# Three pads and a tile shift that set where 256-column moving operands start

## The chip, the core and the metric

The kernel runs on one core of a Trainium2 chip. The metric is device time in microseconds of one execution, from three executions of the kernel; the trace comes from a further execution that was profiled.

## The reference

Retention attention (scores weighted by a decay, no softmax) over 4 batches, 8 heads, 576 positions and 64 dimensions gives 2304 tokens of 512 features. Two MLPs follow. Cut to what matters:

```python
ret = (q @ k.T) / sqrt(64) * Dmat          # Dmat = gamma_h ** (i - j) for i >= j, else 0
x   = (ret @ v)                            # as (2304, 512)
h   = relu(x @ w_in)                       # 512 -> 2048
x   = (h * h) @ w_out                      # 2048 -> 512
g   = x @ w_gate                           # 512 -> 1536
out = (silu(g) * (x @ w_val)) @ moe2_w_out # 1536 -> 512
```

Weights of the MLPs arrive as 64-bit words on the device (the kernel rounds them to float32 itself).

## The kernel before, in words

Every float32 operand of the MLPs is split into a high and a low part, and each product is made of three matmuls in float32r: high weights by high data, high by low, low by high. The helper `three` (L235, L236, L237) issues them; the last MLP's output product (`o_piece`, L1285 to L1287) issues its own three. A matmul here has a stationary operand of 128 columns, that is 512 bytes in each partition, and a moving operand of 512, 384 or 256 columns (2048, 1536 or 1024 bytes in each partition).

The order on TensorE is fixed by a chain (`pe` makes every TensorE step depend on the one before). The stages are:

- 0 to about 148 us: attention chunks among the first token block of the first MLP (512 columns: operands `x`, then `h`).
- about 148 to 219 us: the second token block, which has only 256 tokens: matmuls `hps<-x,w` (`mlp1_h`) and `acc<-h,w` (`mlp1_y`), all of 256 columns, with attention chunks between them.
- to about 470 us: three more token blocks. Their first product is done by a Strassen-like scheme (`mlp1_s`): seven products of 256 columns for each pair of weight tiles (`gv<-xb,w` and `hps<-xb,w`, weights partly from `sx`), with the second product (512 columns, `acc<-h,w`) in pieces between them.
- to the end: the second MLP. Its first two products have 384 columns (`gv<-xc,w`), and between them stand pieces of the output product of 256 columns (`acc<-w,at`, `hps<-w,at`, `gv<-w,at`), where the weight tile is the moving operand and the activations `at` are stationary.

Memory in a partition is handed out by pools in the order in which they are opened, so the width of a pad tile moves all tiles behind it. `pad3` stands ahead of the attention's pools, `pad4` between `xs` and `sx`, and `pad6` between the last MLP's `xc`, `rg` and its `at`. `shift(n)` leaves some floats unused at the front of `x` (L507, in `new_x`) and of `h` (in `mlp1_act`) where a block has fewer than 512 tokens.

In the built program the start of the moving operand minus the start of the stationary one, modulo 512 bytes, is 0 for all float32r matmuls of 512 and 384 columns and 192 for all of 256 columns (192 `x`, 192 `h`, 1008 `xb` and 1134 `w` by `at` matmuls). The first 144 matmuls of the first token block, in pieces of 384 and 128 columns, also start at 0.

Of the kernel before, what the change touches and what calls it, by code (L numbers as in the profile page):

```python
# [10 lines left out]
F32 = mybir.dt.float32  # L11
# [181 lines left out]
def kernel(ctx: ExitStack, tc: tile.TileContext, units, qtab, tab, w1, w2, out):  # L193
# [277 lines left out]
    late, hps_free = {}, {}  # L471
# [1 line left out]


    astack = ExitStack()
    astack.enter_context(tc.tile_pool(name="pad3", bufs=1)).tile([128, 208], F32, name="pad3")
    xp = astack.enter_context(tc.tile_pool(name="xp", bufs=1))
    up = astack.enter_context(tc.tile_pool(name="up", bufs=1))
    ap_ = astack.enter_context(tc.tile_pool(name="ap", bufs=1))
# [19 lines left out]

    def shift(n):  # L500

        return 48 if n < 512 else 0

    def new_x(j):
        n = BLOCKS[j][1] * C
        t = (x1 if j else xp).tile([128, KC * 2 * n + shift(n)], F32R, tag="x", name="x")
        X[j] = t[:, shift(n):].rearrange("p (k a n) -> p k a n", k=KC, a=2)  # L507
# [208 lines left out]
    def mlp1_act(j, f):  # L716
# [16 lines left out]
        def hi():  # L733
            t = hp.tile([128, 2 * n + shift(n)], F32R, tag="h", name="h")
            Hs[j, f] = t[:, shift(n):].rearrange("p (a n) -> p a n", a=2)
            nc.scalar.copy(out=Hs[j, f][:, 0], in_=st["r"])
# [719 lines left out]
    def swap():  # L1456
        astack.close()
        late["tl"] = ctx.enter_context(tc.tile_pool(name="tl", bufs=1, reuse_waits="tile"))
        for key in ("xb", "xs", "pad4", "sx"):
            late[key] = bstack.enter_context(tc.tile_pool(name=key, bufs=7 if key == "xb" else 1, reuse_waits="tile"))  # L1460
        late["pad4"].tile([128, 80], F32, name="pad4")
        late["S"] = late["sx"].tile([128, 2, HALF1], F32R, tag="sx", name="sx")
        pgv = ctx.enter_context(tc.tile_pool(name="pgv", bufs=1, space=PSUM, reuse_waits="tile"))
        late["MA"], late["MB"], more = (pgv.tile([128, 512], F32, name=f"gv{i}") for i in range(3))
        late["more"] = [banks[0], more]

    def swap2():
        wstack.close()
        for key, bufs in (("xc", NX), ("rg", 1), ("pad6", 1), ("at", NAT), ("tm", 1), ("gg", 1)):
            late[key] = ctx.enter_context(tc.tile_pool(name=key, bufs=bufs, side="right", reuse_waits="tile"))  # L1470
        late["pad6"].tile([128, 48], F32, name="pad6")

    def swap3():
        bstack.close()
# [6 lines left out]
    for j in range(PLAIN_BLOCKS):  # L1481
        at = dict(zip(INSERTS[j], range(cell, NC)))
        cell += len(at)
        for f in range(NF1):
# [13 lines left out]
            if c is not None:  # L1498
# [5 lines left out]
                if c + 1 < NC:  # L1504
                    att_load(c + 1, 40)
    do.named["open"] = do("NONE", 0.0, swap, [*(lo_op[c] for c in range(NC)), h_op[0, NF1 - 1], f_last[2], *(st_op[c] for c in range(NC))])
    sum_loads()
    pieces = mlp1_y(*pend, apart=True)
    for j in range(PLAIN_BLOCKS, NB):
        if j > PLAIN_BLOCKS:  # L1510
            fetch_x1(j, -1)
        for p in range(NF1P):
            if p == 1:
                for _ in range(LATER.get(j, 0)):
                    convert2()
            pieces = [*mlp1_s(j, p, pieces), *mlp1_y(j, 2 * p, apart=True), *mlp1_y(j, 2 * p + 1, apart=True)]
    late["open2"] = do("NONE", 0.0, swap2, [y_op[NB - 1, NA - 1], N_op[NB - 1, NA // 2, 5]])
    late["open3"] = do("NONE", 0.0, swap3, [late["open2"], ("ysdone", 0), "lowxs", N_op[NB - 1, NF1P - 1, 6]])
    while todo:
# [3 lines left out]
    for b in range(N2):  # L1523
# [13 lines left out]
        for f in range(NF2):  # L1537
# [9 lines left out]
            n = len(mine)  # L1547
# [94 lines left out]
```

## Time and profile before

| | |
|---|---|
| median of three executions | 862.42 us (862.01 to 864.3) |
| profiled execution, its own time | 866.6 us |
| its span, first to last instruction | 864.8 us |
| TensorE busy share of the span | 99% |
| mean granted TensorE clock | 0.996 |

A matmul's row has a start and a duration; durations overlap, since matmuls are pipelined. What a matmul costs in a dense stream is the distance from its start to the next one's start, called the spacing here. It is read from the timeline as the time between two rows divided by the number of matmuls from one to the other.

### The profile page before, as it was taken

What the parts mean: (1) busy time and instruction counts of PE and PEld (TensorE: products, weight loads), DVE (VectorE), ACT (ScalarE), POOL (GpSimd) and SP (SyncE); (2) the same over time, 40 slices, a digit from 0 to 9 for tenths busy, and PEclk for the clock granted to TensorE, in tenths of its full rate; (3) what the DMA queues carried; (4) which work ended last, traced back from release to release, by engine and by line L of the source; (5) the groups of instructions that cost most, each with busy time, mean ns of one, the idle gap of its engine ahead of it and who ended that gap; (6) DMA issues with size and microseconds to landing.
All of it is one profiled execution on the core that took longest, in us unless ns stands there. A gap on an engine that the chain in (4) does not pass through costs nothing.

```text
span 864.8 us, 15867 instructions
## 1 busy us (share of the span) xinstructions
PE 853.8 (99%) x5990; PEld 804.0 (93%) x5990; DVE 628.0 (73%) x1034; ACT 506.7 (59%) x994; POOL 134.7 (16%) x141
## 2 busy tenths in 40 slices
PE   8999999999999999999999999999999999999998
PEld 6878888989999999999998999999999999999998
DVE  5799987646677857785788778588666688656675
ACT  3577774437877877887887444365333355333353
POOL 3121127651223022212310201000000000000000
PEclk9899999999999999999999999999999999999999
DMA  9587879999989789969899898978867788776782
GB/s 369 206 329 268 305 268 315 387 379 301 316 297 329 267 288 346 315 233 329 281 342 385 300 402 296 392 259 308 318 227 263 261 261 281 276 260 223 267 265 74
DMA packets 113084, 254.83 MB, mean 295 GB/s; under 512 B 8560, under 2 KB 67696, under 8 KB 103664
## 3 DMA queue, kind: packets, MB, share of 16 engines
q1 hardware_dynamic: 113008, 253.82, 83.5%
q8 instruction: 47, 0.77, 0.4%
q14 instruction: 29, 0.24, 0.1%
HBM read 195.59 MB, written 58.20 MB: 293 GB/s over the span
## 4 chain that ended last, share of the span: by engine, by line
PE 92%; DMA 5%; ACT 1%; DVE 1%; issue 0%; SPq 0%; DVEq 0%
PE gv L235 13%; PE gv L237 13%; PE gv L236 13%; PE acc L237 7%; PE acc L236 7%; PE acc L235 7%; PE acc L1285 4%; PE acc L1287 4%; PE acc L1286 4%; PE hps L235 4%; PE hps L237 4%; PE hps L236 4%; PE sc L577 1%; DMA raw<-w 1%; DMA qk<-units 1%; DMA w<-ws 1%
## 5 line engine op out<-in xcount | busy, mean ns | idle before, releaser
L235 PE MATMUL gv<-xc,w 128*128 128x384 f32 x504 | 169.4, 336 | 0.2 <-ACT u L1133 0.2
L237 PE MATMUL gv<-xc,w 128*128 128x384 f32 x504 | 168.9, 335 | 0.0
L236 PE MATMUL gv<-xc,w 128*128 128x384 f32 x504 | 168.7, 335 | 0.0
L236 PE MATMUL acc<-h,w 128*128 128x512 f32 (+1 forms) x320 | 117.3, 367 | 0.0
L237 PE MATMUL acc<-h,w 128*128 128x512 f32 (+1 forms) x320 | 117.3, 367 | 0.0
L235 PE MATMUL acc<-h,w 128*128 128x512 f32 (+1 forms) x320 | 117.3, 367 | 0.0
L453 POOL TENSOR_TENSOR f<-f 128x256 f32<-128x256 f32 x72 | 61.9, 859 | 274.2 <-DVE cw L410 181.5
L235 PEld LDWEIGHTS gv<-xc,w 128*128 128x128 f32 x504 | 94.6, 188 | 1.3 <-ACT u L1133 0.6
L236 PEld LDWEIGHTS gv<-xc,w 128*128 128x128 f32 x504 | 94.6, 188 | 0.1
L237 PEld LDWEIGHTS gv<-xc,w 128*128 128x128 f32 x504 | 94.6, 188 | 0.0
L1287 PE MATMUL acc<-w,at 128*128 128x256 f32 x288 | 81.0, 281 | 0.0
L1285 PE MATMUL acc<-w,at 128*128 128x256 f32 x288 | 80.9, 281 | 0.0
L1286 PE MATMUL acc<-w,at 128*128 128x256 f32 x288 | 80.9, 281 | 0.0
L237 PEld LDWEIGHTS acc<-h,w 128*128 128x128 f32 x320 | 60.1, 188 | 10.0
L235 PE MATMUL gv<-xb,w 128*128 128x256 f32 x238 | 67.1, 282 | 0.0
L237 PE MATMUL gv<-xb,w 128*128 128x256 f32 x238 | 66.8, 281 | 0.0
L236 PE MATMUL gv<-xb,w 128*128 128x256 f32 x238 | 66.8, 281 | 0.0
L236 PEld LDWEIGHTS acc<-h,w 128*128 128x128 f32 x320 | 60.1, 188 | 6.4
L235 PEld LDWEIGHTS acc<-h,w 128*128 128x128 f32 x320 | 60.1, 188 | 6.4
L927 DVE TENSOR_TENSOR h<-g,h 128x256 fp32r<-128x256 f32 x96 | 47.9, 499 | 19.1 <-ACT h L923 18.2
L1145 DVE TENSOR_TENSOR m<-gv,m 128x384 f32<-128x384 f32 x36 | 20.1, 558 | 53.5 <-PE gv L237 53.5
L1133 ACT COPY m<-gv 128x384 f32<-128x384 f32 x72 | 34.5, 479 | 40.7 <-PE gv L237 40.2
(174 smaller groups left out, 2094.9 us busy)
## 6 DMA issues: line engine op xcount, KB each, us to landing
w<-wdS SPq DMA_DIRECT2D x36, 1024.0 KB, 5.5
raw<-w SPq DMA_DIRECT2D x34, 1024.0 KB, 7.5
w<-wdP SPq DMA_DIRECT2D x36, 768.0 KB, 7.3
w<-ws SPq DMA_DIRECT2D x94, 256.0 KB, 5.0
w<-wdOP SPq DMA_DIRECT2D x54, 256.0 KB, 5.4
w<-wdOS SPq DMA_DIRECT2D x18, 768.0 KB, 7.5
ws<-cw SPq DMA_DIRECT2D x16, 512.0 KB, 8.5
wdS<-cw SPq DMA_DIRECT2D x12, 512.0 KB, 6.3
```

The costliest lines, as they stand in the source:

```text
L235: nc.tensor.matmul(ps, lhsT=wh, rhs=xh, start=first, stop=False, skip_group_check=onto)
L236: nc.tensor.matmul(ps, lhsT=wh, rhs=xl, start=False, stop=False, skip_group_check=onto)
L237: nc.tensor.matmul(ps, lhsT=wl, rhs=xh, start=False, stop=last, skip_group_check=onto)
L453: nc.gpsimd.tensor_tensor(out=w[:, o], in0=w[:, x], in1=w[:, y], op=op)
L577: nc.tensor.matmul(s[h][:, p], lhsT=A[c][r, p, 1], rhs=A[c][r, p, 0], start=True, stop=True)
L927: nc.vector.tensor_tensor(out=t[:, 1, half], in0=st[key][:, half], in1=t[:, 0, half].bitcast(F32), op=ALU.subtract)
L1133: nc.scalar.copy(out=st[name], in_=late[bank][:, :HALF])
L1145: nc.vector.tensor_tensor(out=st["m5"], in0=late["MA"][:, :HALF], in1=st["m5"], op=ALU.add)
L1285: nc.tensor.matmul(ps, lhsT=ah, rhs=wh, start=product not in ONTO and q == 0 and off == 0, stop=False, skip_group_check=True)
L1286: nc.tensor.matmul(ps, lhsT=ah, rhs=wl, start=False, stop=False, skip_group_check=True)
L1287: nc.tensor.matmul(ps, lhsT=al, rhs=wh, start=False, stop=q == NQ - 1, skip_group_check=True)
```

## The change

`shift` gives 16 floats (64 bytes) instead of 48 (192 bytes) for blocks of fewer than 512 tokens. `pad3` and `pad4` become 32 floats (128 bytes) longer, `pad6` 32 floats shorter. In the built program every moving operand of 256 columns then starts 64 bytes past its stationary operand modulo 512; the matmuls of 512, 384 and 128 columns keep their difference. Three kinds of tile carry it: the operands `x` and `h` of the second block start 128 bytes earlier in their tiles, `xb` lies 128 bytes lower, and `at` lies 128 bytes higher. With them the result tiles `m1`, `u2`, `m5`, `rs` and `st` move down, and `g` and `sg` up, each by 128 bytes. All instructions stand in the same order on all engines as before, with the same sizes and waits.

```diff
-    astack.enter_context(tc.tile_pool(name="pad3", bufs=1)).tile([128, 208], F32, name="pad3")
+    astack.enter_context(tc.tile_pool(name="pad3", bufs=1)).tile([128, 240], F32, name="pad3")
...
-        return 48 if n < 512 else 0
+        return 16 if n < 512 else 0
...
-        late["pad4"].tile([128, 80], F32, name="pad4")
+        late["pad4"].tile([128, 112], F32, name="pad4")
...
-        late["pad6"].tile([128, 48], F32, name="pad6")
+        late["pad6"].tile([128, 16], F32, name="pad6")
```

## Rows read from the trace of the kernel before

**Rows 1.** The page: engines, busy us (share of the span), instructions.
```profile
PE 853.8 (99%) x5990; PEld 804.0 (93%) x5990; DVE 628.0 (73%) x1034; ACT 506.7 (59%) x994; POOL 134.7 (16%) x141
```

**Rows 2.** Waits of TensorE after 225 us: us in total, times, longest.
```profile
PE gv L235 <- ACT u L1133: 0.2, 1, 0.2
```

**Rows 3.** Stages: window, us, busy (count) by engine, granted clock, DMA share, GB/s.
```profile
148.00:225.00 77.00, 75.53 (x769) 72.25 (x768) 44.57 (x74) 44.04 (x96) 32.54 (x35) 1.00 1.00 351
225.00:473.00 248.00, 247.76 (x1552) 225.10 (x1551) 185.00 (x312) 198.97 (x434) 50.58 (x58) 1.00 0.89 310
473.00:560.00 87.00, 87.00 (x548) 86.71 (x548) 64.91 (x117) 38.69 (x75) 7.82 (x10) 1.00 0.95 346
560.00:865.00 305.00, 301.76 (x2051) 301.27 (x2049) 211.25 (x385) 131.57 (x271) 0.00 (x0) 1.00 0.73 254
```

**Rows 4.** 256-column matmuls by line and shape: count | busy us, mean ns | idle.
```profile
L237 PE MATMUL hps<-x,w 128*128 128x256 f32 x64 | 17.7, 277 | 0.0
L236 PE MATMUL acc<-h,w 128*128 128x256 f32 x64 | 17.7, 277 | 0.0
...
L237 PE MATMUL gv<-xb,w 128*128 128x256 f32 x238 | 66.8, 281 | 0.0
...
L235 PE MATMUL hps<-xb,w 128*128 128x256 f32 x94 | 26.4, 281 | 0.0
...
L1286 PE MATMUL acc<-w,at 128*128 128x256 f32 x288 | 80.9, 281 | 0.0
...
L1287 PE MATMUL hps<-w,at 128*128 128x256 f32 x54 | 15.2, 281 | 0.0
...
L1285 PE MATMUL gv<-w,at 128*128 128x256 f32 x36 | 10.1, 281 | 0.0
```

**Rows 5.** Timeline of TensorE, 256 columns, second block: first and last of 191.
```profile
194.30 0.28 PE L236 MATMUL hps<-x,w 128*128 128x256 f32 x1
...
215.84 0.28 PE L237 MATMUL gv<-xb,w 128*128 128x256 f32 x1
```

**Rows 6.** The same, last MLP: first and last of 101 of 256 columns.
```profile
572.15 0.28 PE L1285 MATMUL acc<-w,at 128*128 128x256 f32 x1
...
583.92 0.28 PE L1286 MATMUL hps<-w,at 128*128 128x256 f32 x1
```

**Rows 7.** The same: 512 columns and the 256 on both sides.
```profile
242.19 0.28 PE L235 MATMUL gv<-xb,w 128*128 128x256 f32 x1
...
242.89 0.39 PE L235 MATMUL acc<-h,w 128*128 128x512 f32 x1
...
244.25 0.28 PE L235 MATMUL hps<-xb,w 128*128 128x256 f32 x1
```

**Rows 8.** The same: 256 columns and 384 behind them, an ordinary place.
```profile
761.49 0.28 PE L1285 MATMUL acc<-w,at 128*128 128x256 f32 x1
...
762.91 0.34 PE L235 MATMUL gv<-xc,w 128*128 128x384 f32 x1
763.08 0.34 PE L236 MATMUL gv<-xc,w 128*128 128x384 f32 x1
...
764.82 0.34 PE L237 MATMUL gv<-xc,w 128*128 128x384 f32 x1
```

**Rows 9.** The same place 10 us later, behind one longer step.
```profile
770.22 0.34 PE L237 MATMUL gv<-xc,w 128*128 128x384 f32 x1
770.39 0.35 PE L235 MATMUL gv<-xc,w 128*128 128x384 f32 x1
770.58 0.34 PE L236 MATMUL gv<-xc,w 128*128 128x384 f32 x1
770.76 0.34 PE L237 MATMUL gv<-xc,w 128*128 128x384 f32 x1
770.93 0.28 PE L1285 MATMUL acc<-w,at 128*128 128x256 f32 x1
...
772.30 0.34 PE L235 MATMUL gv<-xc,w 128*128 128x384 f32 x1
```

## The prediction

> **What bounds the kernel now.** I read the engines' shares first. TensorE is busy for 853.8 of 864.8 us [rows 1], and the reader should see that no other engine comes near it. Then its waits: after 225 us there is one, of 0.2 us [rows 2]. So TensorE's stream sets the end, and what counts is the spacing of its matmuls, from start to start. The granted clock is 1.00 in all four stages behind 148 us [rows 3], which is the level of 2.4 GHz, and so 256 columns alone would take 106.7 ns, 384 would take 160.0 and 512 would take 213.3.
>
> The timeline gives the spacings. In the second block 191 matmuls of 256 columns stand in one unbroken run from 194.30 to 215.84 us, 190 steps: 113.4 ns each [rows 5]. In the last MLP 101 of the same width run from 572.15 to 583.92, 100 steps: 117.7 ns each [rows 6]. I call these the lower and the upper spacing. Both runs start their moving operands 192 bytes past the stationary ones, so this offset alone does not fix the spacing. The profile's mean durations tell the two apart over the whole kernel: 277 ns for the groups of the second block and 281 ns for all large groups behind it [rows 4]. The matmuls of 512 columns take 6 steps from 242.89 to 244.25, 226.7 ns each [rows 7], and those of 384 take 10 steps from 763.08 to 764.82, 174 ns each [rows 8]. Beyond their columns' own time that is 13.4 and 14 ns, at an offset of 0; the 256-column ones pay 6.7 ns at the lower spacing and 11.0 at the upper.
>
> What decides between the two spacings? DMA traffic does not: the lower one stands in the stage where the DMA share is 1.00, the upper one where it is 0.73 [rows 3]. The rows point to the state in which a run is entered. Twelve matmuls from 761.49 to 762.91, entered from an even stream of 384 columns, take 118.3 ns each [rows 8]. Twelve at 770.93 take 114.2 ns [rows 9]; the stream ahead of them was jolted by one step of 190 ns (770.39 to 770.58) where about 174 is usual. Once entered, a spacing stays: 100 steps in a row did not leave the upper one [rows 6]. I read this as two streams, the moving operand's reads and the next weights' reads, that lock into one of two patterns. That reading is inferred, not shown.
>
> **The change part by part.** It adds and removes no instruction, and it moves none past another on any engine or queue. What it changes is where 2526 matmuls read.
>
> First, 1008 matmuls of `xb` and 1134 of `w` by `at`. By their groups' mean durations nearly all run at the upper spacing [rows 4]: three lines of 238, 94, 288, 54 and 36 are 2130 matmuls. About 75 of them still run at the lower spacing (those at the start of the `xb` stage, where the run of [rows 5] ends, and the twelve of [rows 9]), and about 55 of the second block run at the upper one, so I count 2110. If 64 bytes bring these to the lower spacing, 2110 x (117.7 - 113.4) ns = 9.1 us, and with the finer value of the triples, 353.3 against 340 ns (or 13.3 ns a triple, what [rows 6] and [rows 5] give within their rounding), 9.4 us. I take 9.3. All of it lies on the path that sets the end, since TensorE waits for nothing there [rows 2].
>
> Second, the second block's 384 matmuls and the 75 at the start of the next stage, some 390 at the lower spacing already. They can gain nothing that the trace shows and can lose the same step, 390 x 4.4 ns = 1.7 us.
>
> The bounds of the unknown spacing at 64 bytes: below, the lower spacing of 113.4 ns, the nearest row of the same shape [rows 5]. Above, the 13.3 ns beyond the columns that the shapes at an offset of 0 pay [rows 7, 8], which is 120.0 ns; 64 bytes lie nearer to that offset than 192 do. I take the lower one, because the same instructions already run at it in two places and a single jolt was enough to get there [rows 5, 9], so it needs only that the entry from 384 or 512 columns falls otherwise. That is a choice, not a proof.
>
> Third, the cover. If TensorE gains 9.3 us over some 640 us, what feeds it must come 1.5% faster. The narrowest place is 473 to 560 us, with a DMA share of 0.95 [rows 3], where TensorE still waits for nothing [rows 2]; about 160 of the 256-column matmuls lie there, so at most 160 x 4.4 ns = 0.7 us can be given back. VectorE and ScalarE are busy for 185 and 199 of the 248 us of the `xb` stage [rows 3], which leaves more than the gain of some 4 us. The result tiles that move by 128 bytes are read and written by those engines, which are not the bound; I cost that at nothing, with their idle time as the cover, and at most the 0.7 us above if it is gone.
>
> Against the change stands a rule. The Trainium skill, "TensorE: Matmul & The Clock Gate", section "Step-by-step: what each phase is for", says that TensorE has two independent read ports, so that loading the next tile's weights steals nothing from the running matmul. By it no offset between the two operands can matter and the sum is 0. The trace agrees only in part: it has two spacings for one shape at one offset, 113.4 and 117.7 ns, which the rule does not give.
>
> Sum: the profiled execution took 866.6 us, of which 864.8 is span; 866.6 - 9.3 = 857.3. It lies 4.2 us above the median of 862.42. The same difference from the median gives **853.1 us**.
>
> **The rivals.** *Half the gap.* The upper spacing may be a mixture (its triple of 353.3 ns lies two steps of 6.67 ns above 340), and one of the two steps may go: 2110 x 2.2 ns = 4.7 us, so 857.7 us. For it: the sizes 6.7 and 13.4 ns beyond the columns are one and two such steps [rows 5, 7]. Against it: no run of the trace shows 115.5 ns.
>
> *No effect.* Entry and pattern are set by how long the weights of the next matmul have been waiting, not by addresses: a 256-column run behind 512 or 384 columns is then at the upper spacing whatever the offset. For it: at one offset both spacings occur, and every ordinary entry from longer matmuls gives the upper one [rows 7, 8]. Against it: a jolt with no wait at all gave the lower one [rows 9]. It gives 862.4 us, or 864.1 if the second block alone loses its lower spacing. The rule of the two read ports leads to the same time.
>
> *Slower.* 64 bytes lie closer to the point at which both streams read the same place modulo 512, and each weights load then costs the moving stream two steps of 6.67 ns instead of one, as it does at offset 0 for 512 and 384 columns [rows 7, 8]. Then the 2110 go from 117.7 to 120.0 ns, 4.9 us, and the 390 at the lower spacing go up by 6.6 ns, 2.6 us: 862.4 + 7.5 = 869.9 us; 867.3 if only the first happens. It decides wherever the spacing of dense 256-column runs is above 117.7 ns. For it: every row at an offset of 0 pays 13 to 14 ns. Against it: those rows have other widths, and their next weights are loaded long before they end.
>
> **How the numbers follow.** The lower spacing everywhere: 0.28, about 853.1 us. Half the gap: 0.17, about 857.7. No effect, with or without the second block's loss: 0.25, 862.4 to 864.1. Slower: 0.30, 867.3 to 869.9. A time within 0.3% (2.6 us) can't be told from no change in a measurement of this kernel. So faster is 0.28 + 0.17 = 0.45, same 0.25, slower 0.30. The likeliest single case gives the time. The range runs from 852 (the whole gain and 1 us more) to 868, which takes in the milder half of the slower case and leaves out the other, about 0.15, and 0.05 below. Cases of both signs hold most of the chance; the likeliest one's own range is 852 to 855.
>
> **What would show it.** Right: the groups of [rows 4] that now have a mean of 281 ns read 277, a run like that of [rows 6] has 113.4 ns a step, and the rows of 384 and 512 columns keep 174 and 226.7. Half: 115 to 116 ns a step. No effect: 281 and 117.7 again. Slower: durations above 281 ns and about 120 ns a step, in the second block too. The forecast is also wrong, with the mechanism right, if the faster stream finds a wait between 473 and 560 us: TensorE's waits behind 225 us would then be above 0.2 us, with a DMA as the releaser.

## The result, and the profile after

The changed kernel took 870.23 us (869.9 to 870.81, four executions) against 863.36 us (862.01 to 865.36, four) for the kernel before: a ratio of 1.008, with a 95% interval of 1.0062 to 1.0099. It is slower by 0.8%, where 853.1 us had been forecast, and 870.23 lies above the range's upper end of 868.

The two profiled executions stand closer together. They have the same mean granted clock, 0.996, and their spans are 868.5 and 864.8 us, 3.7 us apart. The windows below cut both spans at the same points of the program: the first 256-column matmul of `x`, of `xb`, and the first of `xc`. The columns are the window, its length and TensorE's busy time with its matmuls, the weight loads, VectorE, ScalarE, GpSimd, the granted clock, the DMA share and GB/s. These points lie a few us ahead of the round figures for the stages given above. First the kernel after:

```profile
145.30:213.70 68.40, 67.39 (x690) 64.20 (x689) 39.17 (x60) 34.49 (x70) 31.69 (x31) 1.00 1.00 350
213.70:460.30 246.60, 246.60 (x1568) 223.23 (x1568) 179.65 (x307) 198.29 (x444) 52.55 (x60) 1.00 0.88 302
460.30:868.50 408.20, 404.91 (x2677) 402.49 (x2675) 289.19 (x524) 182.16 (x363) 9.49 (x12) 1.00 0.79 278
```

The kernel before, cut at the same points:

```profile
145.30:212.90 67.60, 66.13 (x691) 63.01 (x690) 37.82 (x60) 34.24 (x70) 31.70 (x33) 1.00 1.01 354
212.90:456.80 243.90, 243.90 (x1568) 222.50 (x1567) 180.32 (x307) 197.92 (x444) 52.37 (x60) 1.00 0.88 304
456.80:864.80 408.00, 404.73 (x2677) 402.30 (x2675) 289.11 (x524) 182.11 (x363) 9.50 (x12) 1.00 0.79 279
```

Both reach the second block at 145.3 us. From there the second block lost 0.8 us, the `xb` stage 2.7 and the last stage 0.2: 3.7 in all. The other engines are busy in each stage for the same time within 1.5 us, the DMA shares agree within 0.01, and behind 225 us TensorE still has the one wait of 0.2 us, as in [rows 2]:

```profile
PE gv L235 <- ACT u L1133: 0.2, 1, 0.2
```

So it is the spacing again. TensorE's timeline of the kernel after: 186 matmuls of the second block and the start of the `xb` stage, answering to [rows 5]; a stretch of the `xb` stage with six matmuls of 512 columns and six of 256, answering to [rows 7]; and 97 matmuls of the last MLP, answering to [rows 6].

```profile
194.08 0.28 PE L236 MATMUL hps<-x,w 128*128 128x256 f32 x1
...
215.87 0.28 PE L235 MATMUL gv<-xb,w 128*128 128x256 f32 x1
...
236.47 0.39 PE L235 MATMUL acc<-h,w 128*128 128x512 f32 x1
...
237.85 0.28 PE L235 MATMUL gv<-xb,w 128*128 128x256 f32 x1
...
238.56 0.39 PE L235 MATMUL acc<-h,w 128*128 128x512 f32 x1
...
575.66 0.28 PE L1285 MATMUL acc<-w,at 128*128 128x256 f32 x1
...
586.97 0.28 PE L1285 MATMUL acc<-w,at 128*128 128x256 f32 x1
```

The first run takes 21.79 us for 185 steps, 117.8 ns each: the second block left the lower spacing for the upper one. The last MLP takes 11.31 us for 96 steps, 117.8 ns: it stayed at the upper one. The six matmuls of 512 columns take 1.38 us, 230 ns each, where [rows 7] has 226.7, although their own operands' offset did not change. The 256-column ones between them take 0.71 us, 118.3 ns.

One stretch of the second block is at the lower spacing even at 64 bytes, 23 matmuls between attention chunks that take 2.49 us, 113.2 ns a step; the other profiles with `x` and `h` at 64 have it too:

```profile
189.24 0.28 PE L236 MATMUL hps<-x,w 128*128 128x256 f32 x1
...
191.73 0.28 PE L237 MATMUL acc<-h,w 128*128 128x256 f32 x1
```

The groups by line and shape (count, busy us, mean ns, idle) show the same for the 512-column matmuls, in two of three lines clearly. After, and behind it one line of before:

```profile
L235 PE MATMUL acc<-h,w 128*128 128x512 f32 x256 | 100.6, 393 | 0.0
L237 PE MATMUL acc<-h,w 128*128 128x512 f32 x256 | 100.5, 393 | 0.0
...
L236 PE MATMUL acc<-h,w 128*128 128x512 f32 x256 | 99.5, 389 | 0.0
...
L237 PE MATMUL hps<-x,w 128*128 128x256 f32 x64 | 17.9, 279 | 0.0
...
L1286 PE MATMUL acc<-w,at 128*128 128x256 f32 x288 | 80.5, 279 | 0.0
```

```profile
L235 PE MATMUL acc<-h,w 128*128 128x512 f32 x256 | 99.6, 389 | 0.0
```

Summing every step of TensorE's timeline beyond its columns' own time gives the shares, after minus before: `x` and `h` of the second block +1.3 us, the 768 matmuls of 512 columns of `h` +2.0 (12.45 against 10.45), `xb` itself +0.6, `xc` +0.3, `w` by `at` -0.1, together 4.1; other steps, waits among them, take 0.4 less. The largest part lies on matmuls that the change doesn't touch, and there on the 546 of 512 columns in the `xb` stage, which go from a mean of 226.7 ns to 230.3; the others keep theirs.

### The profile page after: what moved, and what is told of

Read it like the earlier page. It is cut to its first block, busy times and chain, and to the rows that moved or that the text cites. A ratio compares the mean times of both kernels' runs of the same rounds, so it can differ in the third digit from the quotient of the medians.

```text
span 868.5 us, 15867 instructions
## 1 busy us (share of the span) xinstructions
PE 857.9 (99%) x5990; PEld 806.2 (93%) x5990; DVE 627.6 (72%) x1034; ACT 506.9 (58%) x994; POOL 135.6 (16%) x141
## 4 chain that ended last, share of the span: by engine, by line
PE 93%; DMA 4%; DVE 1%; ACT 1%; issue 1%; SPq 1%; DVEq 0%
PE gv L235 13%; PE gv L237 13%; PE gv L236 13%; PE acc L237 7%; PE acc L235 7%; PE acc L236 7%; PE hps L235 4%; PE acc L1286 4%; PE acc L1287 4%; PE acc L1285 4%; PE hps L237 4%; PE hps L236 4%; PE sc L577 1%; DMA raw<-w 1%; PE xs L617 1%; DMA qk<-units 1%
```

## The experiments

**Theory after the result.** At 64 bytes a dense run of 256 columns keeps the upper spacing and can't reach the lower one from nearly all places where this kernel enters it; the longer matmuls between such runs pay too. *Rival 1:* the time has nothing to do with the offset of the operands, but with the moved result tiles or with how an execution starts. *Rival 2:* the "slower" case of the prediction, 120 ns near an offset of 0 modulo 512, falling with the distance.

**The spacing by itself.** A kernel of its own, which leaves out the model's computation, has TensorE read eight weight pairs in turn and one moving pair in runs of 60 matmuls of 256 columns, at offsets of 0 to 448 bytes in steps of 64. Each run is entered from 512 columns, from 384 and twice after a pause; between them stand four cycles of six matmuls of 512 and six of 256. Its loop, cut to these runs (`triples(n, off, times)` issues three matmuls of n columns for each of its times):

```python
for off in (0, 64, 128, 192, 256, 320, 384, 448):
    triples(512, 0, 2); triples(256, off, 20); triples(512, 0, 2)
    for _ in range(4):
        triples(256, off, 2); triples(512, 0, 2)
    triples(384, 0, 2); triples(256, off, 20); triples(384, 0, 4)
    pause(); triples(256, off, 20); pause(); triples(256, off, 20)
...
```

> A kernel of its own, without the model's computation: runs of 60 float32r matmuls of 256 columns at offsets 0, 64, ... 448 bytes (moving past stationary, modulo 512), entered from 512 columns, from 384 columns and after a pause of TensorE, then 384 and 512 columns at each offset. Theory A (an offset and the state on entry lock the two read streams into a pattern): at 192 the run after a pause has 113.4 ns a step and the run behind 512 or 384 columns 117.7; at 64 all three entries have 117.7, and the 512-column matmuls between short 256-column runs at 64 take over 227 ns. Theory B (the offset alone, costs rise towards 0): 120 ns at 0, 117 to 120 at 64 whatever the entry, lower at 256. Theory C (two independent ports): one spacing for all offsets.

Timeline of TensorE in this kernel, first and last row of each dense run: offset 0 behind 512 columns, 64 behind 512, 64 behind the second pause, 192 behind 512, 192 behind 384.

```profile
18.13 0.28 PE L45 MATMUL b<-x,w 128*128 128x256 f32 x1
...
25.09 0.28 PE L46 MATMUL b<-x,w 128*128 128x256 f32 x1
...
63.12 0.28 PE L45 MATMUL b<-x,w 128*128 128x256 f32 x1
...
70.07 0.28 PE L47 MATMUL b<-x,w 128*128 128x256 f32 x1
...
99.82 0.28 PE L45 MATMUL b<-x,w 128*128 128x256 f32 x1
...
105.71 0.28 PE L46 MATMUL b<-x,w 128*128 128x256 f32 x1
...
152.28 0.28 PE L46 MATMUL b<-x,w 128*128 128x256 f32 x1
...
159.11 0.28 PE L47 MATMUL b<-x,w 128*128 128x256 f32 x1
...
170.04 0.28 PE L46 MATMUL b<-x,w 128*128 128x256 f32 x1
...
176.50 0.28 PE L46 MATMUL b<-x,w 128*128 128x256 f32 x1
```

The steps between those rows are 58, 59, 52, 58 and 57, so the spacings are 120.0, 117.8, 113.3, 117.8 and 113.3 ns. At offset 0 the entry makes no difference. At 64 the run is at the upper spacing behind 512, behind 384 and behind one of two pauses. At 192 it is at the upper one behind 512 columns and at the lower one behind 384 and behind the pauses. The picture repeats every 256 bytes, not every 512: 256 runs as 0 does, 320 as 64, 448 as 192 (but for one pause, behind which 448 is at the upper spacing), and 128 and 384, which are as far from 0 modulo 256 as can be, take 118.7 to 120. Theory A missed in two places: at 192 it had the upper spacing behind 384 columns too, and at 64 behind every pause. That speaks against rival 2: distance from 0 buys nothing steadily, and 64 is not at 120.

The cycles show the neighbours. The first of six matmuls of 512 columns, the first of the six of 256 behind them, and the next of 512, at offset 64 and then at 192:

```profile
74.39 0.39 PE L45 MATMUL b<-x,w 128*128 128x512 f32 x1
...
75.77 0.28 PE L45 MATMUL b<-x,w 128*128 128x256 f32 x1
...
76.48 0.39 PE L45 MATMUL b<-x,w 128*128 128x512 f32 x1
...
163.37 0.39 PE L45 MATMUL b<-x,w 128*128 128x512 f32 x1
...
164.72 0.28 PE L45 MATMUL b<-x,w 128*128 128x256 f32 x1
...
165.43 0.39 PE L45 MATMUL b<-x,w 128*128 128x512 f32 x1
```

A cycle takes 2.09 us at 64 and 2.06 at 192; nearly all of the 0.03 lie in the six matmuls of 512 columns (1.38 and 1.35), as in the kernel. At offset 0 they take 231 ns each. The end of this kernel gives the longer matmuls offsets of their own: 512 columns take 226.7 ns at 0 and 229 to 233 at 64, 128 and 192, 384 columns 173.3 at 0 and 173 to 176 at the others. So an offset of 0 is the best of these for 512 columns and the worst for 256.

**One part of the change at a time.** Three kernels change one set of operands each and leave the other two at 192 bytes. Only the second block's `x` and `h`, by a slice that starts at 16 floats in the unmoved tile (no result tile moves):

```diff
+    def at_front(n):
+        return 16 if n < 512 else 0
...
-        X[j] = t[:, shift(n):].rearrange("p (k a n) -> p k a n", k=KC, a=2)
+        X[j] = t[:, at_front(n):at_front(n) + KC * 2 * n].rearrange("p (k a n) -> p k a n", k=KC, a=2)
...
-            Hs[j, f] = t[:, shift(n):].rearrange("p (a n) -> p a n", a=2)
+            Hs[j, f] = t[:, at_front(n):at_front(n) + 2 * n].rearrange("p (a n) -> p a n", a=2)
```

> Only the second block's x and h start 64 bytes past the weights; xb and at stay at 192. Theory A: the lower spacing there (340 ns a triple) becomes the upper one (353.3), 384 matmuls x 4.4 ns = 1.7 us at most: 1.3 to 1.7 us above before, nothing behind 225 us changes. Theory B': the loss of 6.9 us is spread by count over all 2526 matmuls: 1.0 us.

Only `xb`, by a pad of 96 floats ahead of it and `pad4` shorter behind it:

```diff
+        bstack.enter_context(tc.tile_pool(name="padx", bufs=1, reuse_waits="tile")).tile([128, 96], F32, name="padx")
...
-        late["pad4"].tile([128, 80], F32, name="pad4")
+        late["pad4"].tile([128, 16], F32, name="pad4")
```

> Only xb starts 64 bytes past the weights (ten of its matmuls, those on sx, at 448); x, h and at stay at 192. Theory A: the 512-column matmuls between its pieces go from 680 to 685 ns a triple (2.0 us in all) and xb's own by 0.6 us: 2.6 us above before, and the second block keeps its lower spacing. Theory B': 1008 of 2526 matmuls, 2.7 us, but in xb's own spacing, with 512 columns unchanged.

Only `at`:

```diff
-        late["pad6"].tile([128, 48], F32, name="pad6")
+        late["pad6"].tile([128, 16], F32, name="pad6")
```

> Only at changes, so that the weights moving over it start 64 bytes past it; x, h and xb stay at 192. Theory A: no more than 0.3 us from before, since the two traces have 353.3 ns a triple there in both. Theory B': 1134 of 2526 matmuls, 3.1 us above before.

Measured against the same 25 executions of the kernel before (864.19 us): the second block alone 866.01 us, ratio 1.0019 (0.9997 to 1.0042); `xb` alone 866.87, 1.0043 (1.0022 to 1.0064); `at` alone 865.12, 1.0014 (0.9995 to 1.0033). Each part by itself cannot explain a ratio of 1.008, and none gains. The ratio of 1.008 may itself be the clock's in part, of which more below. The stages say where each lies. Windows as above: second block and `xb` stage with only the second block changed,

```profile
142.50:211.20 68.70, 67.42 (x691) 64.32 (x690) 37.96 (x60) 34.49 (x71) 33.79 (x33) 1.00 0.99 351
211.20:455.70 244.50, 244.20 (x1567) 222.58 (x1567) 180.26 (x307) 197.56 (x444) 52.41 (x60) 1.00 0.89 304
```

and all three stages with only `xb` changed:

```profile
143.80:210.80 67.00, 66.09 (x690) 63.02 (x689) 38.95 (x60) 34.40 (x70) 33.95 (x34) 1.00 1.01 358
210.80:457.30 246.50, 246.50 (x1569) 223.10 (x1568) 180.30 (x307) 198.53 (x444) 52.73 (x60) 1.00 0.88 302
457.30:863.20 405.90, 402.65 (x2677) 400.23 (x2675) 288.98 (x524) 182.01 (x363) 9.51 (x12) 1.00 0.79 280
```

The second block goes from 67.6 to 68.7 where its operands changed and is 67.0 where they did not; the `xb` stage goes from 243.9 to 246.5 only where `xb` changed (the 244.5 in between holds a wait of 0.3 us for VectorE at 324 us). With `xb` alone the 512-column matmuls of this stage take 230.3 ns, as in the kernel after, so Theory B', which left them unchanged, is out. So the loss goes with the operands, part by part. In the first of the three no result tile had moved; with `xb` alone the tiles behind it moved too, but the kernel of runs has no such tiles and shows the same 230 ns. That speaks against rival 1 as the cause of these two terms. With `at` alone the last stage took 408.1 us, as before's 408.0; but with `xb` alone it took 405.9, and there its operands read just as in the kernel before. So this stage varies by 2 us without the change.

**Both kernels once more.** To see what varies by itself, the kernel after and the kernel before, word for word, were run again.

> The changed kernel again, word for word, in more executions, to compare executions that have the same granted clock. Theory A: at equal mean clock it is 4 us (0.5%) above before, as the two traces differ by 4.1 us in TensorE's steps, and it has executions at a clock of 1.0 as often as before has; the rest of the 6.9 us is the draw of the start's clock. Theory C: at equal clock it is 6 to 7 us above, so the trace of before was of an execution with unusually few matmuls at the lower spacing.

> The kernel before, word for word, once more with a profile. Theory A: the second block at 340 ns a triple again; the output product's runs of 256 columns at 353 or, for a stretch, 340 ns, so that two executions of it differ by up to 5 us with the same instructions; if TensorE's clock is at half for none, one or two stretches of 3.4 us at the start, the second block begins near 142, 144 or 145 us.

The kernel after took 868.07 us against 865.05 (12 and 17 executions): 1.0031 (1.0013 to 1.0049), with the same sign as the first comparison and less than half its size. The kernel before took 861.37 us in its profiled execution, 5.2 less than the 866.6 that the prediction started from. Its windows:

```profile
142.20:209.70 67.50, 66.20 (x691) 63.05 (x689) 37.79 (x60) 34.24 (x70) 31.89 (x32) 1.00 1.00 355
209.70:453.70 244.00, 244.00 (x1569) 222.56 (x1568) 180.75 (x307) 198.14 (x444) 52.28 (x60) 1.00 0.89 304
453.70:859.60 405.90, 402.62 (x2677) 400.15 (x2675) 289.02 (x524) 182.22 (x363) 9.50 (x12) 1.00 0.79 281
```

The second block and the `xb` stage repeat within 0.1 us. Two other things moved. The second block began at 142.2 us, not 145.3. And the last stage is 2.1 us shorter: in it, 196 matmuls of `at` in an unbroken run took 22.10 us, 113.3 ns a step, the lower spacing:

```profile
833.83 0.28 PE L1287 MATMUL hps<-w,at 128*128 128x256 f32 x1
...
855.93 0.28 PE L1287 MATMUL acc<-w,at 128*128 128x256 f32 x1
```

Of the 1133 steps behind `at` matmuls, 553 are at 115 ns or less in this execution and 11 in the first one of the same kernel. In the other two profiles with `at` at 192 bytes, those of the second block alone and `xb` alone, 77 and 547 are. In the three with `at` at 64, the kernel after twice and `at` alone, 48, 45 and 49 are. So 64 bytes may cost the `at` runs a gain of 2 us that the kernel before has in some executions and not in others; three profiles are too few to show it, and the executions below give +0.2 us with an interval of 0.8.

The 3 us ahead of the second block are clock. In both executions of the kernel before TensorE waits 1.9 us for VectorE up to 28.5 or 28.3 us:

```profile
PE hps L236 <- DVE x L649: 1.9, 1, 1.9
```

The windows behind that wait, of the first execution and then of the second:

```profile
28.60:35.40 6.80, 6.80 (x33) 5.97 (x34) 3.18 (x6) 3.85 (x5) 0.00 (x0) 0.50 0.67 203
```

```profile
28.60:35.40 6.80, 6.54 (x45) 5.26 (x44) 5.11 (x8) 5.36 (x8) 0.00 (x0) 1.00 0.73 239
```

The granted clock was 0.50 (the level of 1.2 GHz) for 6.8 us in one and 1.00 in the other, behind the same wait. With `xb` alone it was 0.68 and 0.82 in the two halves of this window, and the second block began in between, at 143.8 us. The 512-column `h` matmuls of the first block go the other way: with the same program they take 227.2 ns a step where the clock had fallen and 230.3 where it had not. Why is open.

So 121 executions of these seven kernels were put into one fit: span = a constant + a slope by mean granted clock + one number for each kernel (scatter left over 1.2 us). At equal clock, in us against the kernel before:

| kernel | us | 95% |
|---|---|---|
| after (both times, 16 executions) | +3.9 | 0.7 |
| second block alone | +0.9 | 0.8 |
| `xb` alone | +2.1 | 0.8 |
| `at` alone | +0.2 | 0.8 |
| offset 0 (below) | +8.1 | 1.2 |
| `at` at 32 (below) | 0.0 | 0.8 |

The parts add to 3.2, against 3.9 for the whole. The executions were taken in groups, each with its own of the kernel before. With one more number for each group the kernel after is at +2.9, from its second 12 executions alone, the three parts at +1.4, +2.6 and +0.7 and offset 0 at +7.3, each within about 0.9 (offset 0 1.3). So the sign and the order stand, and the size of the loss is known to about 1 us. By clock the mean spans are, before and after: 864.6 and 868.4 us at 0.996, 861.7 and 866.0 at 1.000. In the first comparison all four executions of the kernel after had 0.996 to 0.998; the second time 5 of 12 had 1.000. So of the 6.9 us between the first medians some 3 to 4 are the offsets. The rest is most likely the clock that these executions happened to get; that is not shown, since the clocks of the four executions of the kernel before are not on record.

**Does the spacing kernel carry over?** It says 120 ns for offset 0. The kernel with all 256-column operands at 0:

```diff
-    astack.enter_context(tc.tile_pool(name="pad3", bufs=1)).tile([128, 208], F32, name="pad3")
+    astack.enter_context(tc.tile_pool(name="pad3", bufs=1)).tile([128, 256], F32, name="pad3")
...
-        return 48 if n < 512 else 0
+        return 0
...
-        late["pad4"].tile([128, 80], F32, name="pad4")
+        late["pad4"].tile([128, 128], F32, name="pad4")
...
-        late["pad6"].tile([128, 48], F32, name="pad6")
```

> All 256-column matmuls at an offset of 0: shift gives 0, pad3 256, pad4 128 floats, no pad6. From the first bench: second block 360 instead of 340 ns a triple (2.5 us), xb 1 ns a matmul more (1.0 us), 512-column matmuls between them about 5 ns each for 576 of them (3 us), weights over at 118.6 to 120 instead of 117.7 (1 to 2.6 us). Theory A: 7.5 to 9 us above before at equal clock. A theory in which 64 costs what 0 costs (both streams near one place): the same time as the changed kernel, 4 us above before.

It took 873.88 us, a ratio of 1.0093 (1.0066 to 1.0121), and is 8.1 us slower at equal clock, inside the 7.5 to 9 expected. Its windows, and the first and last of 215 matmuls of 256 columns from the second block on:

```profile
143.80:213.90 70.10, 68.25 (x690) 65.09 (x689) 38.22 (x60) 34.23 (x71) 32.40 (x32) 1.00 0.97 342
213.90:462.70 248.80, 248.50 (x1569) 224.85 (x1568) 180.21 (x307) 198.41 (x444) 52.15 (x60) 1.00 0.88 299
462.70:872.60 409.90, 406.63 (x2677) 404.24 (x2675) 289.15 (x524) 181.89 (x363) 9.52 (x12) 1.00 0.78 277
```

```profile
193.91 0.28 PE L236 MATMUL hps<-x,w 128*128 128x256 f32 x1
...
219.57 0.28 PE L237 MATMUL gv<-xb,w 128*128 128x256 f32 x1
```

The 214 steps take 25.66 us, 119.9 ns each, as in the kernel of runs. The three stages are 2.5, 4.9 and 1.9 us longer than in before's first profile. So the offset acts on the spacing in this kernel too, and 64 lies between 192 and 0.

**Is there a better offset?** Two more kernels without the model's computation looked for one. The first repeats the runs at 14 offsets from 16 to 240 bytes and adds runs of 12 between runs of 12 of 384 columns.

```diff
-OFFSETS = (0, 64, 128, 192, 256, 320, 384, 448)
+OFFSETS = (16, 32, 48, 64, 80, 96, 112, 144, 160, 176, 192, 208, 224, 240)
...
-        triples(384, 0, 2)
+        triples(384, 0, 4)
+        for _ in range(3):
+            triples(256, off, 4)
+            triples(384, 0, 4)
...
```

> A kernel of its own, without the model's computation, as the first one but with 14 offsets between 16 and 240 bytes, and with short runs of 12 matmuls of 256 columns between runs of 12 of 384. Theory A (the pattern depends on the offset modulo 256 bytes and on the entry): at 192 again 353 ns a triple behind 512 columns and 340 behind a pause, at 64 again 353 and 512-column triples of 685 between; some offset beside 192 may keep 340 behind all entries. Theory B (costs grow steadily towards an offset of 0): the spacing falls steadily from 16 to 128 bytes and rises again to 240.

No order by distance came out. At 112 long runs settle at 113.3 ns behind every entry, but groups of six between longer matmuls take 117.0 and the cycle 2.07 us; at 16 a run takes 113.4 behind 384 columns and 118.7 behind 512; at 144 the cycle takes 2.06, but long runs take 116.7 ns or more. At 192 the first kernel's readings repeat; at 64 both pauses now lead to the upper spacing. Nothing is clearly below 192 in the mix that this kernel has. The second moves the weights instead of the moving operand, as the last MLP does, between groups of 384 columns:

```diff
+    def pieces(by, times):
...
+            k = by // 4 + i % 3 * 128
+            m = i % 4 * 256
+            ah, al = (x[:, a, k:k + 128] for a in range(2))
+            wh, wl = (w[:, a, m:m + 256] for a in range(2))
...
+    for by in SHIFTS:
+        triples(384, 0, 6)
+        for n, m in ((4, 2), (3, 2), (4, 4), (3, 2), (1, 2), (4, 4)):
+            pieces(by, n)
+            triples(384, 0, m)
...
+        pause()
+        pieces(by, 12)
...
```

> A kernel of its own, without the model's computation: as in the last MLP, short runs of 256-column matmuls whose moving operand starts at 0 modulo 512 and whose stationary one is shifted by 0, 16, ... 240 and 320 bytes, between runs of 384 columns at an offset of 0. Theory A (the entry from 384 columns differs from the first benches', since here the weights shift and not the moving operand): at a shift of 320 (an offset of 192) the short runs hold both 340 and 353 ns a triple, as in the traces of the kernel before and of the one with only xb changed. If the shift of either operand is the same: 340 at 320 and at 64 throughout, as at 192 in the second bench.

Moving the stationary operand up by 192 bytes gives an offset (moving minus stationary) of 320, which is 64 modulo 256, and moving it by 320 gives 192. TensorE's timeline behind a pause, at these two offsets in this order:

```profile
487.80 0.28 PE L66 MATMUL b<-w,x 128*128 128x256 f32 x1
...
491.10 0.28 PE L64 MATMUL b<-w,x 128*128 128x256 f32 x1
...
633.78 0.28 PE L64 MATMUL b<-w,x 128*128 128x256 f32 x1
...
636.96 0.28 PE L65 MATMUL b<-w,x 128*128 128x256 f32 x1
```

That is 28 steps each, 117.9 ns at 64 and 113.6 at 192. Behind 384 columns both are at the upper spacing throughout; Theory A had both spacings among the short runs at 192. So one offset and one width ahead do not fix the spacing either: at 192 behind 384 columns it is 113.3 ns in the two kernels that move the moving operand and 117.7 in this one, and why is open. It fits the last stage in so far as 192 can fall either way, while 64 modulo 256 has the upper spacing alone here. The best behind 384 columns was 116.7 ns, with offsets of 48 and 32 modulo 256 between the operands, so 32 was put into the kernel, for `at` alone:

```diff
-        late["pad6"].tile([128, 48], F32, name="pad6")
+        late["pad6"].tile([128, 8], F32, name="pad6")
```

> The kernel before with pad6 of 8 floats, so that only the weights moving over at start 32 bytes past it; x, h and xb stay at 192. From the bench with shifted weights: 116.7 to 116.8 ns a step at 32 whatever the entry, against 117.7 at 192 behind 384 columns and 113.3 where the lower spacing is met. Theory A: the last stage is 1134 x 1.0 = 1.1 us shorter than in an execution of before that is at the upper spacing throughout, and 1 us longer than in one that meets the lower one for half its length; the median at equal clock is within 1 us of before and varies less. If the offset alone set the price, steadily falling towards 192 or 256: slower than before by 1 us or more.

It took 865.62 us against 865.59 (12 and 17 executions), a ratio of 1.0005 (0.9987 to 1.0022): no difference. The long `at` runs did take 116.7 ns a step; in its profile the `at` steps together took 1.0 us less than in before's first profile and 1.4 us more than in its second. No version was found that beats the kernel before.

## Why the prediction was wrong

**What bounds the kernel** was right: TensorE's stream sets the end, the change moved only its spacing, and no wait, transfer or other engine came up in its place. The cover of the third part was not called on.

**The step that failed first** is "I take the lower one", between the bounds of 113.4 and 120.0 ns for the spacing at 64 bytes. The runs show 117.8 from the entries that this kernel has, in the second block, the last MLP and the kernel of runs alike; 113.3 came only in the one stretch at 189 us and behind some pauses. The reason given was that the same instructions already run at the lower spacing in two places. Both stand at 192 bytes [rows 5, 9], the very offset that was to go, so they said nothing about 64. The term was put at 9.3 us and gave nothing: `xb` lost 0.6 us and `at` moved by 0.1 between the two profiles.

**The second step that failed** is that the change concerns 2526 matmuls and that "the rows of 384 and 512 columns keep 174 and 226.7". The 512-column ones between the `xb` pieces went to 230.3 ns and cost 2.0 us, more than any other term. No rival had that. The sum put this term at nothing because those matmuls keep their own offset; the runs show that their neighbours' offset counts too.

**The second part was right in place and near in size**: the second block and what follows "can lose the same step", 1.7 us. It named this loss and left it out of its sum. The block's matmuls lost 1.3 us by their steps, and the part alone 0.9 +/- 0.8 at equal clock.

**The start of the sum** was weak. It took one execution's last stage and its 4.2 us above the median as the kernel's own. The second profile of before shows that 3 us of such a difference can be the clock at 28 us and 2 us the pattern that the `at` runs fall into. Of the 2110 matmuls said to run at the upper spacing, some 540 of `at` ran at the lower one in that execution, without any change.

**The rivals.** *Slower* had the sign, and its 867.3 to 869.9 us lie just below the median measured. That nearness is in part luck, for the second median is 868.07 us. And its mechanism is not what happened: it put 120.0 ns on all dense runs, by nearness modulo 512. The runs have 120 at 0 and 256 (and up to 120 at 128 and 384), not at 64, and at equal clock the loss is 3.9 us against its 4.9 to 7.5. Its point against itself, that a 512-column matmul's next weights are loaded long before it ends, is weak too: in the trace of before such a load takes 0.19 us and starts with the matmul, whose spacing is 0.23. *No effect*, in the form in which only the second block loses its lower spacing, was nearest in the spacings that it foresaw; it lacked the neighbours' 2.0 us, and its reason, that addresses do not count, is contradicted by the scan of offsets. *Half the gap* needed 115.5 ns, which the kernel after does not show.

**The rule that was weighed.** The Trainium skill, "TensorE: Matmul & The Clock Gate", section "Step-by-step: what each phase is for", gives TensorE two independent read ports, so that loading the next weights takes no read bandwidth from the running matmul. The traces disagree with what the prediction drew from it, that no offset can count: behind 384 columns, with nothing but the offset changed, runs of 60 matmuls settle at 113.3, 117.7 or 120.0 ns each.

**Still open.** That the reads of weights and moving operand get in each other's way is inferred from the offsets; no run shows a read. Why the picture repeats at 256 bytes is not known, nor why the neighbours of 512 columns pay at 64. Nor is it known what makes the `at` runs of one program take the lower spacing in one execution and not in the next; the three profiles with `at` at 64 have almost none, and whether another execution has can't be told. What draws the clock behind the wait at 28 us was not tried.

## What to carry to other kernels

An offset between operands that pays in one place says nothing about another offset: measure the spacing over a scan of offsets, in runs entered as the kernel enters them and with its longer matmuls in between, since those can pay more than the runs themselves. Before a gain of 1% is worked out from one profile, take a second one of the same kernel and cut both into stages: what differs there is not the kernel's to give. Compare stages, and spans at equal granted clock, rather than medians of a few executions.

## What the runs showed of the hardware

- Dense runs of 256-column float32r matmuls, each with a weight load of its own, take 113 to 120 ns a step. At offsets of 0, 64 and 192 bytes modulo 256 they take 120.0, 117.7 (113.3 behind some pauses and in one stretch behind attention) and 113.3 or 117.7; offsets between give other values, 116.7 at 32. At some offsets it depends on what was ahead of the run, and it can differ from one execution of a program to the next.
- Matmuls of 512 columns, their own offset unchanged, take a step of 226.7 ns between 256-column ones at 192 bytes (five profiles of the kernel) and 230.3 at 64 (three). In the first block, with no such neighbours, they took 227.2 or 230.3 from one execution to the next.
- The profile's mean durations are no sure sign: the second block after the change has a mean of 279 ns at a spacing of 117.8, where [rows 4] has 281 for runs at 117.7.
- The same program with the same 1.9 us wait went on at a granted clock of 0.50 for 6.8 us in one execution and at 1.00 in another, worth 3 us of the span.
